# Two-queue head loads, PSUM-fed VectorE products, a later back transform and 490-wide tiles in a convolution-plus-MLP kernel

## The chip, the cores and the metric

The kernel runs on one core of one Trainium2 chip. The metric is the device time of the launch in microseconds. The engines are named as in the profile: PE (TensorE), DVE (VectorE), ACT (ScalarE), POOL (GpSimd), SP (SyncE, which here only issues DMAs). SBUF is the on-chip memory and PSUM the accumulator memory that PE writes, with banks of 512 fp32 values per partition.

## The reference

```python
def _attn_ref(x, v, pos_emb, w1, w2):          # x, v: (2, 12480, 128); pos_emb: (12480, 64)
    h_mlp = np.maximum(pos_emb @ w1, 0.0) @ w2
    window = np.exp(-0.01 * pos)[:, None]
    h_filt = h_mlp * window
    u = x * v
    Uf = np.fft.rfft(u, n=2 * S, axis=1)
    Hf = np.fft.rfft(h_filt, n=2 * S, axis=0)
    y = np.fft.irfft(Uf * Hf[None], n=2 * S, axis=1)[:, :S, :]
    return x * y

h = attn_out.reshape(24960, 128) @ w_in        # w_in: (128, 2048)
out = np.maximum(0.01 * h, h) @ w_out          # w_out: (2048, 128)
```

A causal convolution of length 12480 over 2 batches and 128 channels, gated by x, feeds an MLP over 24960 tokens. The large MLP weights arrive as float64.

## The kernel before

**MLP.** Each fp32 product is made from three fp32r matmuls of a high and a low part. A token tile (up to `WIDE` = 512 columns) runs `NF` = 16 steps over the hidden dimension. One step, called an iteration here, is `m1` (three matmuls into PSUM tile `mh`), the activation on ACT (`rh`) and the remainder on DVE (`rl`), and three steps later `m2` (three matmuls into `acc`). Tiles are 392 wide once, then 512, and two of 252 at the end: 50 tiles, 800 iterations. `mh` has three buffers.

**Convolution.** It is done as staged Fourier matmuls on 8 units (b, j): 2 batches times 4 blocks of the sequence, in the order (0,0), (1,0), (0,1), (1,1), (0,2), (1,2), (0,3), (1,3). Units with b = 0 also transform the filter. Each unit has two phases:

- `ConvA`: loads of x, v and pos_emb; POOL forms `uh` = x·v; PE transforms it in bursts; the result is copied out of PSUM and stored to a DRAM scratch `scr1`.
- `ConvB`, in 7 chunks (the last one small): load of `bin` from `scr1`; `up` (PE) makes the spectrum of u; for b = 0, `ep` and `hp` (PE) and `esg` (POOL) make the filter's spectrum; `mac` multiplies complex spectra, one term for j = 0, two for j = 1 and 3, five for j = 2; `dp` (PE) transforms the sum `pin` back, ACT copies it to `ct`, and it goes to scratch `scr2`. Spectra that later units need go through DRAM (`u`, `g`, `p`, loaded as `sp`).

A `mac` term is two 1024-wide products `t` of spectra in SBUF, one on POOL and one on DVE, an add of the earlier terms to the first on POOL where there are any, and a 512-wide difference (POOL) and sum (DVE) into `pin` or `pp`. `up` is therefore first copied from PSUM to `us` in SBUF by ACT. `dp` of chunk c-1 stands right after `up` and `hp` of chunk c.

**Fronts.** For each of 64 blocks of 392 tokens (384 in the last sequence block), `front` loads `cin`, makes y with matmuls (`yp`), gates it on DVE (`zt`), transposes it (`zp`), copies it on ACT to `zf` and then to `zh`, and POOL makes the low part `zl`. `finish` transposes the result back (`op`) and stores it.

**Order.** The Tile scheduler is off: each engine runs its instructions in program order. Unit (0,0) runs alone in a head, together with the conversion of the float64 weights (`from_float64`, `weights`). The other seven units are cut into pieces, and `pace` strews the pieces over the iterations: `cost` weighs the units, `windows` and `knots` turn the weights into an iteration range for each, and a piece is emitted when the iteration count has come that far. PE runs piece and iteration matmuls in one order, so a piece that waits holds back what stands behind it.

In the main part all conv matmuls use two PSUM banks, and a piece takes both:

```python
def pair():
    return psc["bank"](), psc["bank"]()
```

## Time and profile before

| | before |
|---|---|
| median of 3 runs | 2089.12 us (2085.14 to 2090.6) |
| profiled execution | 2086.52 us, span 2084.6 us |
| PE busy | 1793.9 us, 86% of the span |
| DVE, POOL, ACT busy | 1054.1, 960.2, 859.9 us |
| first `m1` matmul | 187.18 us |
| DMA | 290.61 MB, mean 139 GB/s |

The profiled execution's time is the span plus 1.92 us around it. The span falls into five stretches, cut where a unit's pieces begin: the head (unit (0,0) and weights, 0 to 187 us), the early units (1,0), (0,1), (1,1) to 729 us, the two units with j = 2 to 1424 us, the late units (0,3), (1,3) to 1869 us, and a tail with no convolution left.

### The profile page before, as it was taken

How to read it: one execution, taken by the hardware profiler on the slowest of the kernel's cores; microseconds unless marked ns; L12 is line 12 of the kernel's file. 1: busy time of each engine (PE TensorE's matmuls, PEld its weight loads, DVE VectorE, ACT ScalarE, POOL GpSimd, SP SyncE). 2: the span in 40 equal slices, each digit the busy share in tenths (PEclk: the TensorE clock that was granted, in tenths of full speed). 3: DMA queues.
4: the chain of work that ended last, by engine and by line, in shares of the span. 5: the costliest groups of instructions: out<-in, count | busy, mean ns of one | idle time of the engine just before them, and what ended most of it. 6: DMA issues, size and time to landing. Idle time of an engine off the chain costs nothing. (4 is left out here: it accounts for less than half of the span.)

```text
span 2084.6 us, 27982 instructions
## 1 busy us (share of the span) xinstructions
PE 1793.9 (86%) x9734; PEld 1258.0 (60%) x9734; DVE 1054.1 (51%) x1482; ACT 859.9 (41%) x1675; POOL 960.2 (46%) x618
## 2 busy tenths in 40 slices
PE   4566999998999899767779777769998899999999
PEld 3334767755676576444457444547765577667788
DVE  2673444455456444544454465555444445545665
ACT  1233544444444444222224232324443344445666
POOL 3232232166426511777773578872166624840000
PEclk9977999999999999887789888779999999999999
DMA  4685574566457454434425453433555356621100
GB/s 121 195 259 148 156 207 126 171 211 206 121 185 213 129 151 150 151 114 134 128 65 143 139 157 108 121 88 108 164 175 176 111 140 193 200 83 43 47 24 16
DMA packets 214034, 290.61 MB, mean 139 GB/s; under 512 B 30061, under 2 KB 138477, under 8 KB 213893
## 3 DMA queue, kind: packets, MB, share of 16 engines
q1 hardware_dynamic: 213893, 288.82, 46.5%
q8 instruction: 77, 1.26, 0.3%
q14 instruction: 64, 0.52, 0.1%
HBM read 181.23 MB, written 107.51 MB: 139 GB/s over the span
## 5 line engine op out<-in xcount | busy, mean ns | idle before, releaser
L745 DVE SCALAR_TENSOR_TENSOR rl<-mh,rh 128x512 fp32r<-128x512 f32 (+1 forms) x672 | 455.6, 685 | 545.7 <-ACT rh L744 545.3
L744 ACT ACTIVATE rh<-mh 128x512 fp32r<-128x512 f32 (+1 forms) x672 | 401.3, 597 | 490.8 <-PE mh L740 475.3
L738 PE MATMUL mh<-zh,w_in_h 128*128 128x512 f32 (+2 forms) x800 | 362.6, 453 | 73.4 <-DVE rl L745 72.2
L739 PE MATMUL mh<-zl,w_in_h 128*128 128x512 f32 (+2 forms) x800 | 319.9, 400 | 0.0
L740 PE MATMUL mh<-zh,w_in_l 128*128 128x512 f32 (+2 forms) x800 | 319.7, 400 | 0.0
L762 PE MATMUL acc<-rh,w_out_h 128*128 128x512 f32 (+2 forms) x800 | 318.8, 399 | 0.0
L763 PE MATMUL acc<-rl,w_out_h 128*128 128x512 f32 (+2 forms) x800 | 318.3, 398 | 0.0
L765 PE MATMUL acc<-rh,w_out_l 128*128 128x512 f32 (+2 forms) x800 | 318.0, 397 | 0.0
L731 POOL TENSOR_TENSOR zl<-zf,zh 128x392 fp32r<-128x392 f32 (+39 forms) x111 | 79.5, 731 | 487.4 <-ACT zh L730 487.1
L738 PEld LDWEIGHTS mh<-zh,w_in_h 128*128 128x128 f32 x800 | 154.1, 193 | 215.7 <-DVE rl L745 102.5
L432 PE MATMUL cv<-pin,mi 64*128 64x512 f32 (+1 forms) x416 | 133.9, 758 | 109.8 <-POOL pin L420 109.4
L420 POOL TENSOR_TENSOR pin<-t 128x512 f32<-128x512 f32 (+1 forms) x112 | 160.4, 1432 | 123.3 <-DVE t L416 107.4
L421 DVE TENSOR_TENSOR pin<-t 128x512 f32<-128x512 f32 (+1 forms) x112 | 87.6, 782 | 185.7 <-POOL t L418 176.0
L740 PEld LDWEIGHTS mh<-zh,w_in_l 128*128 128x128 f32 x800 | 155.6, 194 | 35.4
L763 PEld LDWEIGHTS acc<-rl,w_out_h 128*128 128x128 f32 x800 | 154.7, 193 | 36.1 <-DVE rl L753 0.2
L762 PEld LDWEIGHTS acc<-rh,w_out_h 128*128 128x128 f32 x800 | 154.9, 194 | 35.5
L765 PEld LDWEIGHTS acc<-rh,w_out_l 128*128 128x128 f32 x800 | 154.3, 193 | 35.8
L415 POOL TENSOR_TENSOR t<-us,sp 128x1024 f32<-128x1024 f32 (+1 forms) x63 | 139.4, 2212 | 63.0 <-ACT us L401 35.7
L739 PEld LDWEIGHTS mh<-zl,w_in_h 128*128 128x128 f32 x800 | 156.7, 196 | 16.6 <-DVE zl L731 0.3
L181 POOL TENSOR_TENSOR uh<-xt,vt 113x512 f32<-113x512 f32 x64 | 81.9, 1286 | 182.4 <-DMA vt<-in_v_dram 50.6
L432 PEld LDWEIGHTS cv<-pin,mi 64*128 64x128 f32 x416 | 46.3, 232 | 164.9 <-POOL pin L420 125.9
L436 ACT COPY ct<-cv 128x512 f32<-128x512 f32 (+1 forms) x104 | 53.7, 565 | 218.5 <-PE cv L432 213.8
(110 smaller groups left out, 2339.5 us busy)
## 6 DMA issues: line engine op xcount, KB each, us to landing
sp<-g SPq DMA_DIRECT2D x72, 512.0 KB
cin<-scr SPq DMA_DIRECT2D x64, 392.0 KB
scr<-ct SPq DMA_DIRECT2D x96, 256.0 KB
sp<-u SPq DMA_DIRECT2D x48, 512.0 KB
scr<-sp SPq DMA_DIRECT2D x128, 147.0 KB
bin<-scr SPq DMA_DIRECT2D x24, 768.0 KB
scr<-sp SPq DMA_DIRECT2D x64, 196.0 KB
xt<-in_x_dram SPq DMA_DIRECT2D x128, 96.0 KB
```

Of the source, the lines that this page charges most:

```text
L415: G(out=t1, in0=u, in1=g[:, 0:1, :].to_broadcast([R, 2, w]), op=ALU.mult)
L420: G(out=acc[:, 0], in0=t1[:, 0], in1=t2[:, 1], op=ALU.subtract)
L421: V(out=acc[:, 1], in0=t1[:, 1], in1=t2[:, 0], op=ALU.add)
L432: nc.tensor.matmul(p[jo][:, :w], mi2[rows, ri, :], pin[rows, ri, :w], start=(ri == 0), stop=(ri == 1))
L738: nc.tensor.matmul(hp, w_in_h[:, fs], zh, start=True, stop=False)
L739: nc.tensor.matmul(hp, w_in_h[:, fs], zl, start=False, stop=False)
L740: nc.tensor.matmul(hp, w_in_l[:, fs], zh, start=False, stop=True)
L744: nc.scalar.activation(out=rh, in_=hp, func=AF.Relu)
L745: nc.vector.scalar_tensor_tensor(out=rl, in0=hp, scalar=0.0, in1=rh, op0=ALU.max, op1=ALU.subtract)
L762: nc.tensor.matmul(ap, w_out_h[:, f, :], rh, start=(f == 0), stop=False)
L763: nc.tensor.matmul(ap, w_out_h[:, f, :], rl, start=False, stop=False)
L765: nc.tensor.matmul(ap, w_out_l[:, f, :], rh, start=False, stop=last and k >= LEAKY)
```

## The change

- **Tiles.** A tile is now made of whole groups of 98 (96 for j = 3) tokens, five to a tile: 392, then 490, for j = 3 480, and 192 at the end. There are 52 tiles and 832 iterations, with the same token columns in all.
- **Products.** The terms whose first factor is the fresh `up` (`first`: one, or two for j = 2) read it from PSUM: DVE does both products, POOL both halves of the join. In the remaining terms (`rest`) both factors are in SBUF: POOL does both products, and POOL the join, but for j = 2, where DVE does the sum. `us` is copied only where it is saved (j < 2).
- **PSUM.** A conv use takes one tile of two banks with one buffer in the main part (three in the head), and it is copied out by one ACT copy.
- **Back transform.** `dp(c-1)` stands behind the first rest term of chunk c (behind the first terms if there is no rest); `pin` has two buffers.
- **Fronts.** `zf` is gone: ACT copies `zh` from PSUM, and DVE makes `zl` from PSUM.
- **Loads.** `ConvA` loads x, v and pos_emb in granules of 8 positions instead of 4 (4, 12 and 16 in the head), into tiles that `ConvB` uses otherwise; one store for a burst instead of two. In the head a second queue, that of ACT, issues about 28 of the loads; the saves of `u` and `g` of unit (0,0) are kept back: six are issued in its chunks 4 to 6, the other eight behind the loads for the first fronts.
- **Pace.** New `cost`, and fewer pieces for most units. By the kernel's own arithmetic the iteration ranges of the stretches go from 233 (early), 227 (j = 2), 192 (late) and 148 (tail) to 202, 290, 200 and 140.
- **Instructions.** DMA issues of SP go from about 1494 to 1185.

```diff
+                self.granules = granules or [(8 * i, 8) for i in range(4)]
+                self.alloc = alloc or self.shared
...
+                i0, n = self.granules[g]
+                t = {}
+                for kind, src, d in (("p", pos_emb, FO), ("x", x[self.b], D), ("v", v[self.b], D)):
+                    if kind != "p" or self.hid:
+                        t[kind] = self.alloc(kind, g, n).rearrange("a (i d) -> a i d", d=d)
+                        load_tokens(t[kind], src, self.j, i0, n, q.get(kind, nc.sync))
+                self.got.append(t)
...
             def burst(self, c, i0, n):
                 e, r = self.e, rows_of(self.j)
                 uh = self.uh[c]
-                a = pair()
+                a = psc["pair"]().rearrange("p (w n) -> p w n", w=2)[:2 * KA]
...
-                o = spt(turn[0] % 4, [128, 1024])[:2 * KA, :2 * n * e].rearrange("k (w i e) -> k w i e", w=2, e=e)
+                o = spt(turn[0] % 5)[:2 * KA, :2 * n * e].rearrange("k (i w e) -> k w i e", w=2, e=e)
...
+                    m0 = 2 * (c * NI + i0)
+                    nc.sync.dma_start(out=scr1[self.b, self.j][m0:m0 + 2 * n].rearrange("m k e -> k m e"),
+                                      in_=o.rearrange("k w i e -> k i w e").rearrange("k i w e -> k (i w) e"))
...
+                self.first = [(g(0), "y")] + ([(g(1), "p")] if j == 2 else [])
+                self.rest = {0: [], 1: [(u(0), g(1), "y")], 3: [(u(0), g(3), "y")],
+                             2: [(u(1), g(1), "y"), (u(1), g(2), "p"), (u(0), g(2), "y")]}[j]
...
             def up(self, c):
...
-                us = self.env("us", [128, 2, 512], 1)
-                for ri in range(2):
-                    nc.scalar.copy(us[:R, ri, :w], p[ri][:R, :w])
                 if self.j < 2:
-                    self.late.append(lambda: nc.sync.dma_start(
-                        out=spec["u", self.b, self.j][c][:R, :1024].rearrange("p (r w) -> p r w", r=2)[:, :, :w],
-                        in_=us[:R, :, :w]))
-                return us
-
...
-                G, V = nc.gpsimd.tensor_tensor, nc.vector.tensor_tensor
-                G(out=t1, in0=u, in1=g[:, 0:1, :].to_broadcast([R, 2, w]), op=ALU.mult)
-                V(out=t2, in0=u, in1=g[:, 1:2, :].to_broadcast([R, 2, w]), op=ALU.mult)
+                    us = self.tile("us", 1024).rearrange("p (r w) -> p r w", r=2)
+                    nc.scalar.copy(us[:R, :, :w], p[:R, :, :w])
+                    self.save(("u", self.b, self.j), c, us)
+                return p[:R, :, :w]
+
+            def t01(self, c):
+                R, w = self.dims(c)
+                return [cpt(f"t{i}", 1024).rearrange("p (r w) -> p r w", r=2)[:R, :, :w] for i in range(2)]
+
+            def mult(self, c, eng, u, g):
+                R, w = self.dims(c)
+                t = self.t01(c)
+                for i in range(2):
+                    eng.tensor_tensor(out=t[i], in0=u[:R, :, :w], in1=g[:R, i:i + 1, :w].to_broadcast([R, 2, w]),
+                                      op=ALU.mult)
...
+            def join(self, c, t, acc, init, im):
+                R, w = self.dims(c)
+                G = nc.gpsimd.tensor_tensor
                 if init is not None:
-                    G(out=t1, in0=t1, in1=init[:R, :, :w], op=ALU.add)
-                yield
-                G(out=acc[:, 0], in0=t1[:, 0], in1=t2[:, 1], op=ALU.subtract)
-                V(out=acc[:, 1], in0=t1[:, 1], in1=t2[:, 0], op=ALU.add)
-                yield
+                    G(out=t[0], in0=t[0], in1=init[:R, :, :w], op=ALU.add)
+                G(out=acc[:R, 0, :w], in0=t[0][:, 0], in1=t[1][:, 1], op=ALU.subtract)
+                im(out=acc[:R, 1, :w], in0=t[0][:, 1], in1=t[1][:, 0], op=ALU.add)
 
...
-                p = pair()
+                p = psc["pair"]().rearrange("p (j w) -> p j w", j=2)
...
+                ct = cpt("ct", KC * D).rearrange("p (k d) -> p k d", d=D)
+                nc.scalar.copy(ct.rearrange("p (j h) d -> p j (h d)", j=2)[:, :H, :w], p[:, :H, :w])
...
-                    us = self.up(c)
-                    vals = {"U": us}
...
-                    if c >= 1:
-                        self.dp(c - 1, pin)
...
+                    acc = {"y": cpt("pin", 1024, 2).rearrange("p (r w) -> p r w", r=2)}
...
+                    rest = [o for t in self.rest for o in t[:2]]
+                    u = self.up(c)
+                    if self.defer and c > 3:
+                        for _ in range(2):
+                            self.defer.pop(0)()
+                    for i, (g, a) in enumerate(self.first):
+                        t = self.mult(c, nc.vector, u, vals[g])
                         yield
-                    pin = acc["y"]
+                        self.join(c, t, acc[a], init[a], nc.gpsimd.tensor_tensor)
+                        init[a] = acc[a]
+                        if i + 1 == len(self.first):
+                            self.load_bins(c + 2)
+                            if self.hid:
+                                if c + 1 < NCH:
+                                    self.ep(c + 1)
+                                    self.load_es(c + 2)
+                                yield
+                            if not self.rest:
+                                free(rest)
...
+                        t = self.mult(c, nc.gpsimd, vals[u], vals[g])
+                        yield
+                        self.join(c, t, acc[a], init[a],
+                                  nc.vector.tensor_tensor if self.j == 2 else nc.gpsimd.tensor_tensor)
+                        init[a] = acc[a]
+                        free([o for t in self.rest[i + 1:] for o in t[:2]])
+                        yield
+                        if i == 0 and c:
+                            self.dp(c - 1, pins.pop(c - 1))
+                            yield
+                    if not self.rest and c:
...
+                grain = [(0, 4), (4, 12), (16, 16)]
...
+                load_t(0, NI, (nc.sync, nc.scalar))
+                a0.load({"p": nc.scalar, "v": nc.scalar})
...
+                a0.load({"v": nc.scalar})
+                load_t(NI, 16 - NI, (nc.sync, nc.scalar))
...
+                a0.load({"v": nc.scalar})
...
+            load_front(0)
+            load_front(1)
+            for f in defer:
+                f()
...
-        psc["bank"] = psc["single"] = lambda: ps.tile([128, 512], F32, tag="cv", name="cv", bufs=2)
+        psc["pair"] = lambda: ps.tile([128, 1024], F32, tag="cv", name="cv", bufs=1)
+        psc["bank"] = psc["single"] = lambda: psc["pair"]()[:, :512]
...
+        groups = [(t, i) for t in range(total) for i in range(NI)]
+        cuts = list(range(NI, len(groups), GROUPS))
+        tiles = [groups[a:b] for a, b in zip([0] + cuts, cuts + [len(groups)])]
+        widths = [sum(size[t] // NI for t, _ in g) for g in tiles]
...
-            zf = sm.tile([128, 2 * NI * KA], F32, tag="zf", name="zf", bufs=1)
-            nc.scalar.copy(zf[:, :n].rearrange("p (i w a) -> p i w a", w=2, a=rows),
-                           zp.rearrange("p i (w a) -> p i w a", w=2)[:, :, :, :rows])
...
+                src = zp[:, i0:i0 + m].rearrange("p i (w a) -> p i w a", w=2)[:, :, :, :rows]
+                nc.scalar.copy(zh, src)
+                nc.vector.tensor_tensor(out=zl, in0=src, in1=zh, op=ALU.subtract)
...
-        cost = [0, 100, 125, 125, 170, 170, 140, 140]
+        cost = [0, 80, 110, 110, 215, 215, 125, 125]
```

POOL's rows in a full chunk of unit (0,2) before, from `esg` to the third term's join (`us` is the fresh spectrum, `sp` and `hs` other spectra, `t` the products):

```order
L356 TENSOR_TENSOR esg<-es,esp 128x4x64
L358 TENSOR_TENSOR esg<-es,esp 128x4x64
L415 TENSOR_TENSOR t<-us,sp 128x1024
L420 TENSOR_TENSOR pin<-t 128x512
L415 TENSOR_TENSOR t<-us,sp 128x1024
L731 TENSOR_TENSOR zl<-zf,zh 128x200
L731 TENSOR_TENSOR zl<-zf,zh 128x192
L420 TENSOR_TENSOR pp<-t 128x512
L415 TENSOR_TENSOR t<-sp 128x1024
L418 TENSOR_TENSOR t<-t,pin 128x1024
L420 TENSOR_TENSOR pin<-t 128x512
```

and after, from the joins of the two first terms to the second rest term's products:

```order
L425 TENSOR_TENSOR pin<-t_6805,t_6806 128x512
L426 TENSOR_TENSOR pin<-t_6805,t_6806 128x512
L425 TENSOR_TENSOR pp<-t_6833,t_6834 128x512
L426 TENSOR_TENSOR pp<-t_6833,t_6834 128x512
L363 TENSOR_TENSOR esg<-es,esp 128x4x64
L365 TENSOR_TENSOR esg<-es,esp 128x4x64
L416 TENSOR_TENSOR t_6900<-sp 128x1024
L416 TENSOR_TENSOR t_6901<-sp 128x1024
L424 TENSOR_TENSOR t_6900<-t_6900,pin 128x1024
L425 TENSOR_TENSOR pin<-t_6900,t_6901 128x512
L416 TENSOR_TENSOR t_6952<-sp,hs 128x1024
L416 TENSOR_TENSOR t_6953<-sp,hs 128x1024
```

The products of the two first terms are gone from POOL, which joins both in four 512-wide operations; of the rest terms it does two products each; `zl` is gone from it.

PE's rows of unit (1,1) before, from `up` of a chunk (L397) to `dp` of the chunk before it (L432):

```order
L397 MATMUL cv<-bin,mb 64x512 x4
L738 MATMUL mh<-zh,w_in_h 128x512
L739 MATMUL mh<-zl,w_in_h 128x512
L740 MATMUL mh<-zh,w_in_l 128x512
L762 MATMUL acc<-rh,w_out_h 128x512
L763 MATMUL acc<-rl,w_out_h 128x512
L765 MATMUL acc<-rh,w_out_l 128x512
L432 MATMUL cv<-pin,mi_91 128x512 x4
```

and after, the rows between that end with `dp` (L436); `up` stands above them, parted from them by one more iteration and a front's `yp`:

```order
L766 MATMUL mh<-zl,w_in_h 128x490
L767 MATMUL mh<-zh,w_in_l 128x490
L789 MATMUL acc<-rh,w_out_h 128x490
L790 MATMUL acc<-rl,w_out_h 128x490
L792 MATMUL acc<-rh,w_out_l 128x490
L765 MATMUL mh<-zh,w_in_h 128x490
L766 MATMUL mh<-zl,w_in_h 128x490
L767 MATMUL mh<-zh,w_in_l 128x490
L789 MATMUL acc<-rh,w_out_h 128x490
L790 MATMUL acc<-rl,w_out_h 128x490
L792 MATMUL acc<-rh,w_out_l 128x490
L436 MATMUL cv<-pin,mi_91 128x512 x4
```

One iteration stood between `up` and `dp`; now there are three.

## Rows read from the trace of the kernel before

**Rows 1.** Windows: length; busy PE, PEld, DVE, ACT, POOL; PE clock, DMA share, GB/s.

```profile
0.00:187.00 187.00, 102.53 (x642) 60.11 (x642) 95.90 (x184) 47.23 (x107) 62.61 (x61) 0.85 0.61 181
187.00:729.00 542.00, 515.27 (x2919) 360.23 (x2920) 272.31 (x363) 246.99 (x474) 227.21 (x155) 0.98 0.59 173
729.00:1424.00 695.00, 545.99 (x2664) 370.22 (x2663) 340.51 (x419) 227.90 (x435) 431.35 (x242) 0.86 0.41 125
1424.00:1869.00 445.00, 420.03 (x2379) 295.86 (x2378) 220.17 (x297) 200.70 (x386) 227.21 (x142) 0.98 0.51 155
1869.00:2084.60 215.60, 210.06 (x1135) 171.63 (x1134) 125.22 (x222) 137.09 (x274) 11.82 (x18) 1.00 0.12 34
```

**Rows 2.** Timeline of POOL over one chunk of unit (0,2).

```profile
1001.17 0.74 POOL L356 TENSOR_TENSOR esg<-es,esp 128x256 f32<-128x256 f32 x1 [5.37 <-ACT es L348]
...
1002.56 2.40 POOL L415 TENSOR_TENSOR t<-us,sp 128x1024 f32<-128x1024 f32 x1
...
1014.15 3.40 POOL L415 TENSOR_TENSOR t<-sp 128x1024 f32<-128x1024 f32 x1
...
1017.63 2.38 POOL L418 TENSOR_TENSOR t<-t,pin 128x1024 f32<-128x1024 f32 x1
...
1020.09 1.78 POOL L420 TENSOR_TENSOR pin<-t 128x512 f32<-128x512 f32 x1
...
1043.56 2.37 POOL L415 TENSOR_TENSOR t<-us,sp 128x1024 f32<-128x1024 f32 x1
```

**Rows 3.** Timeline of POOL, start of two successive chunks of unit (1,2).

```profile
1278.33 2.35 POOL L415 TENSOR_TENSOR t<-us,sp 128x1024 f32<-128x1024 f32 x1
...
1319.77 2.35 POOL L415 TENSOR_TENSOR t<-us,sp 128x1024 f32<-128x1024 f32 x1
```

**Rows 4.** Timeline of DVE in the chunk of rows 2.

```profile
1002.69 3.34 DVE L416 TENSOR_TENSOR t<-us,sp 128x1024 f32<-128x1024 f32 x1
...
1014.11 1.23 DVE L416 TENSOR_TENSOR t<-sp 128x1024 f32<-128x1024 f32 x1 [0.57 <-POOL pp L420]
```

**Rows 5.** Timeline of POOL, start of two successive chunks of unit (0,1).

```profile
462.45 2.41 POOL L415 TENSOR_TENSOR t<-us,sp 128x1024 f32<-128x1024 f32 x1
...
481.65 2.41 POOL L415 TENSOR_TENSOR t<-us,sp 128x1024 f32<-128x1024 f32 x1
```

**Rows 6.** Timeline of PE in the same chunk of unit (0,1), conv matmuls.

```profile
467.30 1.94 PE L397 MATMUL cv<-bin,mb 128*64 128x512 f32 x8
...
470.77 1.15 PE L374 MATMUL cv<-w,esg 64*64 64x128 f32 x32
...
475.80 1.99 PE L432 MATMUL cv<-pin,mi 64*128 64x512 f32 x8 [1.88 <-POOL pin L420]
...
478.45 1.09 PE L345 MATMUL cv<-mb,bin 128*64 128x128 f32 x16 [0.67 <-ACT ct L436]
```

**Rows 7.** Timeline of PE in the tail, one matmul of two successive iterations.

```profile
2046.04 0.40 PE L739 MATMUL mh<-zl,w_in_h 128*128 128x512 f32 x1
...
2047.44 0.40 PE L739 MATMUL mh<-zl,w_in_h 128*128 128x512 f32 x1
```

**Rows 8.** Groups by line, the matmuls of the fronts.

```profile
L715 PE MATMUL yp<-cin,gt 98*64 98x128 f32 x1024 | 72.3, 285 | 10.3 <-DMA cin<-scr 10.3
...
L722 PE MATMUL zp<-ident,zt 113*128 113x113 f32 x256 | 36.6, 266 | 0.8 <-DVE zt L717 0.8
```

**Rows 9.** Timeline of PE in the head.

```profile
52.69 0.61 PE L188 MATMUL cv<-ident,pos 113*128 113x113 f32 x2 [7.88 <-DMA pos<-in_pos_emb_dram]
...
182.28 1.98 PE L715 MATMUL yp<-cin,gt 98*64 98x128 f32 x16 [10.29 <-DMA cin<-scr]
```

**Rows 10.** Timeline of POOL in the head.

```profile
55.70 1.26 POOL L181 TENSOR_TENSOR uh<-xt,vt 113x512 f32<-113x512 f32 x1 [10.50 <-DMA vt<-in_v_dram]
```

**Rows 11.** Groups by form, two 512-wide DVE operations.

```profile
L753 DVE TENSOR_TENSOR rl<-sp,rh 128x512 fp32r<-128x512 f32 x96 | 66.7, 695 | 44.8 <-ACT rh L752 43.1
...
L717 DVE TENSOR_TENSOR zt<-yp,xm 113x512 f32<-113x512 f32 x64 | 43.9, 687 | 28.3 <-PE yp L715 27.1 <-DMA sp<-u 0.4 <-DMA scr<-sp 0.4
```

More of the change, by code (lines that the diff above doesn't have):

```diff
@@ L28 @@
 PAD = 1088
+GROUPS = 5
 @with_exitstack
@@ L136, in tile_conv_mlp @@
     psc = {}
-    def pair():
-        return psc["bank"](), psc["bank"]()
     with tc.manual_schedule():
@@ L148, in tile_conv_mlp, with spt, cpt, __init__ @@
         turn = [0]
[L150 to L151 removed]
+        def spt(i):
+            return cp.tile([128, 1024], F32, tag=f"sp{i}", name="sp")
+        kept = {}
+        for tag, n in (("us", 1024), ("hs", 1024), ("pp", 1024), ("ct", 1024), ("esp", 512), ("esg", 512)):
+            kept[tag] = const.tile([128, n], F32, name=tag)
+            nc.gpsimd.memset(kept[tag][32:64], 0.0)
+        def cpt(tag, n, bufs=1):
+            if tag in kept:
+                return kept[tag]
+            return cp.tile([128, n], F32, tag=tag, name=tag, bufs=bufs)
         class ConvA:
[L155 removed]
+            def __init__(self, b, j, granules=None, alloc=None, evac=None):
                 self.b, self.j = b, j
@@ L231, in run, with body @@
-            def run(self):
-                while self.loaded < 2:
-                    self.load()
-                first = self.prep(0)
-                for _ in first if self.hid else first or ():
+            def body(self):
+                if self.hid and self.j:
+                    load_win(self.j, nc.sync)
+                for i in range(2):
+                    if len(self.got) < 1 + i:
+                        self.load()
+                    yield
+                for _ in self.prep(0):
@@ L289, in __init__ @@
-                self.fresh = fresh
-                self.terms = terms
-                self.loads = []
-                if j == 3:
-                    self.loads.append(("p", b))
-                for t in terms:
-                    for o in t[:2]:
-                        if o not in ("U", fresh) and o not in self.loads:
-                            self.loads.append(o)
-                self.sp = {}
-            def pieces(self):
-                per = (4 if self.hid else 2) + 2 * len(self.terms)
-                return self.WAIT + 1 + NCH * per + 2
+                self.after, self.defer = after, defer
@@ new lines, in __init__, with dims @@
+                self.loads = [("p", b)] if j == 3 else []
+                for o in [t[0] for t in self.first] + [o for t in self.rest for o in t[:2]]:
+                    if o != self.fresh and o not in self.loads:
+                        self.loads.append(o)
+            def pieces(self):
+                per = (2 if self.hid else 0) + 2 * len(self.first) - 1 + 2 * len(self.rest) + 1
+                return self.WAIT + 1 + NCH * per + 3
+            def dims(self, c):
+                _, n, h = chunk(c)
+                return (128 if n > 1 else 64), h * D
@@ L431, in dp @@
                         rows = slice(64 * jo, 64 * jo + 64)
-                        nc.tensor.matmul(p[jo][:, :w], mi2[rows, ri, :], pin[rows, ri, :w],
+                        nc.tensor.matmul(p[:, jo, :w], mi2[rows, ri, :], pin[rows, ri, :w],
                                          start=(ri == 0), stop=(ri == 1))
-                ct = self.env("ct", [128, KC, D], 1)
-                for jo in range(H):
-                    nc.scalar.copy(ct[:, jo * h:jo * h + h, :].rearrange("p k d -> p (k d)"), p[jo][:, :w])
+                ct = cpt("ct", KC * D).rearrange("p (k d) -> p k d", d=D)
+                nc.scalar.copy(ct.rearrange("p (j h) d -> p j (h d)", j=2)[:, :H, :w], p[:, :H, :w])
                 def store():
@@ L670, in tile_conv_mlp, with headtile @@
+            hb = st.enter_context(tc.tile_pool(name="hb", bufs=1, reuse_waits="tile"))
+            defer = []
+            def headtile(tag, n):
+                return hb.tile([128, n], F32, tag=tag, name=tag, bufs=5)
+            nc.vector.tensor_scalar_mul(mi2, mi2, 4.0)
+            b0 = ConvB(0, 0, after=conv_a[1, 0].load, tile=headtile, defer=defer)
+            for i, _ in enumerate(b0.run()):
+                for _ in range(4 if i < 7 else 3):
+                    next(wprep, None)
                 if i == 12:
@@ L778, in finish @@
             whole = []
-            for t in range(total):
-                for kk, a, c, n in pieces_of(t):
+            for t in sorted({t for t, _ in tiles[k]}):
+                n = size[t] // NI
+                for kk, a, i0, m in parts[t]:
                     if kk == k:
@@ L800, in tile_conv_mlp @@
         ZB, DEEP = 3, 3
-        first = [next(pieces_of(t))[0] for t in range(total)]
+        first = [parts[t][0][0] for t in range(total)]
         ends, e = {}, NTL * NF
@@ L877, in do @@
                 next(fronts[t])
-        load_front(0)
-        load_front(1)
+        for _ in range(4):
+            step()
         run(front(0))
```

437 lines of the change are left out of this document (190 added, 247 removed).

## The prediction

> **What bounds the kernel now.** I read the windows first [rows 1]. [...] In the head PE works 103 of 187 us, no engine is full, and the DMA share is 0.61.
>
> POOL's timeline shows what holds j = 2 back. A full chunk of unit (0,2) starts with `esg`, and its first product starts 41.0 us before that of the next chunk [rows 2]; in unit (1,2) the distance is 41.4 us [rows 3]. The reader should look at the product times. POOL's takes 2.40 us at the chunk's start and 3.40 us later, and the DVE product of a pair takes 3.34 us where POOL came first and 1.23 us where DVE came first [rows 2, 4]. So two products from SBUF on these engines do not overlap; the second waits for the first. A term costs the sum of both engines' products, whoever has them. In the head, the rows to see are waits on loads: 7.88 us for `pos`, 10.50 us for `vt`, 10.29 us for `cin` [rows 9, 10].
>
> **Tiles.** An iteration 512 wide takes 1.40 us on PE [rows 7], so 1.34 us at 490 columns and 1.31 at 480. A front adds (72.3 + 36.6) / 64 = 1.70 us [rows 8], and the transposes of a finish are as many as those of `zp`, 0.57 us: 2.27 us for 392 tokens, 0.19 us for an iteration of 512 and 0.18 for one of 490. That makes 1.59 us before and 1.52 (j = 3: 1.49) after. All columns together stay the same, so the width costs nothing as such. It matters where iterations lie: the j = 2 stretch, in which PE waits anyway, takes 290 of them and not 227.
>
> - Early: 233 × 1.59 = 370 against 202 × 1.52 = 307, so 63 us less.
> - Late: 192 × 1.59 = 305 against 200 × 1.49 = 298, 7 us less: 438.
> - Tail: 116 × 1.40 and 32 of 252 columns at 0.69, 184.5, against 124 × 1.31 and 16 of 192 columns at 0.53, 171: 13.5 us less, 202.
>
> **j = 2.** `t0` and `t1` have one buffer each, so DVE's two products of a first term wait for POOL's last join and POOL's join waits for them: a chain over both engines.
>
> - A rest term: two POOL products at 2.37, the add 2.38, the difference with DVE's sum ahead of it 1.78 [rows 2, 3], 8.90 us; three make 26.7.
> - A first term: two products on DVE, then two 512-wide operations on POOL. No row has a product from PSUM. Its lower bound is the 1.23 us of the same product from SBUF [rows 4]; its upper bound is the 2.40 us that POOL takes. I take 1.23, since a 512-wide DVE operation takes 0.687 us with an operand in PSUM (`zt`) and 0.695 with both in SBUF [rows 11]. POOL's 512-wide operations are half of 2.37 each. So 2.46 + 2.37 = 4.83; two make 9.7.
> - `esg` twice 0.74 [rows 2], for b = 0 alone: 1.5.
>
> A chunk takes 37.8 us in unit (0,2) and 36.4 in (1,2), against 41.0 and 41.4; six full chunks each save 19 + 30 = 49 us. PE alone would need less: 12 pieces per chunk at 144.9 iterations / 130 pieces is 13.4 iterations or 20.4 us, and 6.2 us of conv matmuls [rows 6]. Outside these chunks more iterations lie: before, 57 of 141 pieces and 38 of 110 at 113.3 iterations for each unit, 85 iterations; after, 58 of 130 and 39 of 99 at 144.9, 122. That is 85 × 1.59 = 135 against 122 × 1.52 = 185, 50 us more. So 695 - 49 + 50 = 696 us: the stretch stays as long, with 63 more iterations in it.
>
> [...]
>
> **Early units.** A full chunk of unit (0,1) takes 19.2 us [rows 5]; PE alone 8 pieces at 0.84 iterations, 10.7 us, and 6.2 us of conv matmuls [rows 6], 16.9. The rest is the wait of `dp` for `pin` (1.88 us) and of `ep` for PSUM (0.67), on PE with iterations queued behind. After, `dp` stands two iterations further back and finds `pin` done. But POOL's chain becomes two products, add and join, 4.74 + 2.38 + 2.37, a first term, 4.83, and `esg`, 1.5: 15.8 us, while PE needs 6 × 0.84 × 1.52 + 6.2 = 13.9. The loss of 2 us stays. In (1,1), without `esg`, `hp` and `ep`, the chain is 14.3 us against 4 × 1.30 × 1.52 + 3.9 = 11.8 of PE, and before it was 6 × 1.23 × 1.59 + 3.9 = 15.6 of PE: a new loss of 2.5 us, 15 for six chunks. In (1,0) the eight saves kept back, 4 MB, run beside its loads; at the stretch's rate, 173 GB/s at a share of 0.59, a full DMA moves 293 GB/s, so they cost 0 to 14 us; I take 7. Early: 542 - 63 + 15 + 7 = 501.
>
> `zl` on DVE and the missing `zf` I cost at nothing: in these stretches DVE is busy half the time and ACT less [rows 1]. If that cover is gone, 0.7 us for each of some 100 pieces comes back.
>
> **Head.** Fewer, larger loads on two queues and fronts loaded ahead of the saves go at the three waits, 28.7 us together; there are shorter ones beside them, and ACT must first issue its share of loads before its first copy. Bounds: nothing (the data come no sooner) and 45. I take 30, near the three waits: 157.
>
> **Sum.** 157 + 501 + 696 + 438 + 202 = 1994 us of span, 1996 with the 1.92 us around it. The median of the runs lay 2.6 us over the profiled time, so 1999 us.
>
> **Rivals.**
>
> - *POOL is freed further.* If DVE's products ran beside POOL's rest terms, a chunk with j = 2 would fall to POOL's own 32.9 us (26.7 + 4.7 + 1.5): 12 × 4.9 = 59 us less, 1940; a head 15 us shorter still would give 1925. For it speaks that operations with a PSUM operand, such as `rl`, do not stretch in these rows; against it that the single `t` buffers tie the engines.
> - *Loads don't gain.* The head stays at 187, and the saves cost their 14 us: 2036; with light chunks 2 us longer than reckoned, 2065. For it: the DMA share of the head is already 0.61 as a mean. Against it: the waits are for few, small, early transfers.
> - *The single PSUM tile.* Every conv use waits in PE's order until the use before it has been copied out or multiplied; before, the first bank was free half a copy earlier, and `up` was released by ACT, not by DVE behind its `rl`. Outside the full j = 2 chunks there are some 190 uses; at 0.5 us of PE wait each 95 us come back, so from 0.5 us it is slower than before; at 0.6 us 2113. For it: `ep` already waits 0.67 us for `ct` [rows 6]. Against it: one or more iterations, 1.5 us each, lie between pieces in most places.
> - *No change.* The saving of 95 us goes to several of these at once and the time stays at 2089.
>
> **Chances.** What I forecast, 1965 to 2035: 0.55. POOL freed: 0.18. Loads don't gain, 2035 to 2080: 0.15. The PSUM tile: 0.08. No change: 0.04. So faster by over 0.3% (about what a measurement of this kernel can tell from no change) 0.88, within it 0.04, slower 0.08. The range 1930 to 2060 leaves out the low end of the second case, the top of the third, and the last two.
>
> **What would show it.** First `m1` matmul near 157 us. POOL's chunk starts in the j = 2 units 36 to 38 us apart, with gaps of 2.5 us while DVE multiplies, and DVE's products at 1.23 us. PE busy at above 95% in the other stretches, and no wait of `dp` for `pin` there. The forecast is wrong if the chunk distance is far from 37, if PE waits for DVE's products or ACT's copies at conv pieces over 0.5 us each, or if the product from PSUM takes nearer 2.4 us: then 48 × 1.17 = 56 us come back.

## The result, and the profile after

The changed kernel takes 2024.67 us (median of 4 runs, 2022.74 to 2026.45), 0.970 of the time before (95% interval 0.968 to 0.971). The forecast was 1999 us, in a range of 1930 to 2060.

The head of the page of the changed kernel, with the clock of PE in 40 slices:

```profile
span 2023.2 us, 27361 instructions
## 1 busy us (share of the span) xinstructions
PE 1760.4 (87%) x9932; PEld 1302.7 (64%) x9932; DVE 901.2 (45%) x1435; ACT 819.1 (40%) x1459; POOL 901.6 (45%) x608
...
PEclk9976989999999999888989998899999999999999
```

The span is 61 us shorter, 2023.2 against 2084.6, and PE is busy 87% of it. Where the time went is read from windows cut as in [rows 1] (length; busy time of PE, PEld, DVE, ACT, POOL; clock, DMA share, GB/s). The head ends with the first `m1` matmul, the other stretches with the last `dp` of a unit:

```profile
0.00:192.80 192.80, 104.83 (x643) 62.65 (x643) 98.28 (x183) 45.12 (x79) 58.43 (x64) 0.87 0.58 163
192.80:699.80 507.00, 457.23 (x2646) 324.04 (x2647) 197.82 (x293) 214.22 (x358) 205.43 (x148) 0.96 0.60 183
699.80:1387.30 687.50, 590.00 (x3151) 442.55 (x3149) 298.04 (x456) 248.43 (x445) 425.87 (x255) 0.92 0.43 131
1387.30:1817.10 429.80, 409.03 (x2403) 303.05 (x2401) 183.08 (x277) 182.92 (x324) 211.84 (x142) 0.99 0.53 160
1817.10:2023.20 206.10, 199.31 (x1098) 170.44 (x1096) 123.98 (x230) 128.45 (x253) 0.00 (x0) 1.00 0.13 36
```

Against 187, 542, 695, 445 and 215.6 us before: the main part gives 67 us, and the head takes 5.8 us more. In the j = 2 stretch PE is now busy 590 us and not 546, at a clock of 0.92 and not 0.86. In the early stretch it is busy 457 of 507 us, 90%, against 95% before.

POOL in a full chunk of unit (0,2) of the changed kernel, to hold against [rows 2]:

```profile
882.82 1.78 POOL L425 TENSOR_TENSOR pin<-t,t 128x512 f32<-128x512 f32 x1
...
887.82 1.29 POOL L425 TENSOR_TENSOR pin<-t,t 128x512 f32<-128x512 f32 x1 [3.22 <-DVE t L416]
889.07 1.28 POOL L426 TENSOR_TENSOR pin<-t,t 128x512 f32<-128x512 f32 x1
...
894.17 1.27 POOL L425 TENSOR_TENSOR pp<-t,t 128x512 f32<-128x512 f32 x1 [3.82 <-DVE t L416]
...
897.34 0.74 POOL L365 TENSOR_TENSOR esg<-es,esp 128x256 f32<-128x256 f32 x1
898.04 4.70 POOL L416 TENSOR_TENSOR t<-sp 128x1024 f32<-128x1024 f32 x2
902.71 2.37 POOL L424 TENSOR_TENSOR t<-t,pin 128x1024 f32<-128x1024 f32 x1
905.16 1.78 POOL L425 TENSOR_TENSOR pin<-t,t 128x512 f32<-128x512 f32 x1
```

and DVE in the same chunk:

```profile
885.32 2.36 DVE L416 TENSOR_TENSOR t<-cv,sp 128x1024 f32<-128x1024 f32 x2 [0.70 <-POOL pin L425]
...
891.75 2.35 DVE L416 TENSOR_TENSOR t<-cv,sp 128x1024 f32<-128x1024 f32 x2
```

Two joins (1.27 to 1.29 us each half), each behind a gap of 3.2 to 3.8 us in which DVE multiplies (two products in 2.36 us), then `esg`, then rest terms without a gap (two products 4.70, add 2.37, difference 1.78). This is the chain that the forecast added up, with gaps longer than its 2.46 us.

### The profile page after: what moved, and what is told of

Its sections match the earlier page's. It is cut to its first block, busy times and chain, and to the rows that moved or that the text cites. A ratio compares the mean times of both kernels' runs of the same rounds, so it can differ in the third digit from the quotient of the medians.

```text
span 2023.2 us, 27361 instructions
## 1 busy us (share of the span) xinstructions
PE 1760.4 (87%) x9932; PEld 1302.7 (64%) x9932; DVE 901.2 (45%) x1435; ACT 819.1 (40%) x1459; POOL 901.6 (45%) x608
## 3 DMA queue, kind: packets, MB, share of 16 engines
q8 instruction: 78, 1.28, 0.3%
## 4 chain that ended last, share of the span: by engine, by line
PE 58%; POOL 20%; DVE 8%; issue 7%; DMA 3%; ACT 2%; SPq 1%; ACTq 0%; POOLq 0%; DVEq 0%
POOL t L416 10%; PE mh L765 8%; PE mh L767 6%; PE mh L766 6%; PE acc L790 6%; PE acc L792 6%; PE acc L789 6%; PE cv L224 4%; POOL t L424 4%; PE cv L400 4%; DVE t L416 3%; PE cv L436 3%; PE yp L744 2%; POOL pin L425 2%; POOL pin L426 2%
## 5 line engine op out<-in xcount | busy, mean ns | idle before, releaser
L772 DVE SCALAR_TENSOR_TENSOR rl<-mh,rh 128x490 fp32r<-128x490 f32 (+3 forms) x704 | 458.8, 662 | 603.7 <-ACT rh L771 601.7
L771 ACT ACTIVATE rh<-mh 128x490 fp32r<-128x490 f32 (+3 forms) x704 | 406.4, 579 | 503.1 <-PE mh L767 483.7
L765 PE MATMUL mh<-zh,w_in_h 128*128 128x490 f32 (+4 forms) x832 | 367.1, 441 | 66.9 <-DVE rl L772 66.2
L766 PE MATMUL mh<-zl,w_in_h 128*128 128x490 f32 (+4 forms) x832 | 323.4, 389 | 0.0
L767 PE MATMUL mh<-zh,w_in_l 128*128 128x490 f32 (+4 forms) x832 | 323.2, 389 | 0.0
L790 PE MATMUL acc<-rl,w_out_h 128*128 128x490 f32 (+4 forms) x832 | 321.8, 387 | 0.0
L789 PE MATMUL acc<-rh,w_out_h 128*128 128x490 f32 (+4 forms) x832 | 321.0, 386 | 0.0
L792 PE MATMUL acc<-rh,w_out_l 128*128 128x490 f32 (+4 forms) x832 | 320.9, 386 | 0.0
L765 PEld LDWEIGHTS mh<-zh,w_in_h 128*128 128x128 f32 x832 | 161.5, 194 | 195.1 <-DVE rl L772 92.0
L425 POOL TENSOR_TENSOR pin<-t,t 128x512 f32<-128x512 f32 (+1 forms) x112 | 142.4, 1272 | 258.8 <-DVE t L416 250.8
L416 POOL TENSOR_TENSOR t<-sp 128x1024 f32<-128x1024 f32 (+1 forms) x84 | 178.1, 2141 | 9.6 <-issue 6.9
L789 PEld LDWEIGHTS acc<-rh,w_out_h 128*128 128x128 f32 x832 | 161.7, 194 | 26.7
L792 PEld LDWEIGHTS acc<-rh,w_out_l 128*128 128x128 f32 x832 | 160.8, 193 | 26.5
L400 PE MATMUL cv<-bin,mb 128*64 128x512 f32 (+1 forms) x416 | 109.4, 638 | 17.2 <-ACT hs L386 12.6
L436 PE MATMUL cv<-pin,mi 64*128 64x512 f32 (+1 forms) x416 | 109.3, 631 | 14.2 <-DVE t L416 13.1
```

What stands on the lines that cost most here:

```text
L400: nc.tensor.matmul(p[64 * jo:64 * jo + 64, ri, :w].rearrange("p (k d) -> p k d", d=D), mb[:, ri, :], t[:, jo * h:jo * h + h, self.off:], s ...
L416: eng.tensor_tensor(out=t[i], in0=u[:R, :, :w], in1=g[:R, i:i + 1, :w].to_broadcast([R, 2, w]), op=ALU.mult)
L425: G(out=acc[:R, 0, :w], in0=t[0][:, 0], in1=t[1][:, 1], op=ALU.subtract)
L765: nc.tensor.matmul(hp, w_in_h[:, fs], zh, start=True, stop=False)
L766: nc.tensor.matmul(hp, w_in_h[:, fs], zl, start=False, stop=False)
L767: nc.tensor.matmul(hp, w_in_l[:, fs], zh, start=False, stop=True)
```

## Experiments

All are edits of the changed kernel; each was timed against the kernel before, in 4 runs. Unit lengths, in us, run from one unit's last `dp` matmul to the next unit's, (1,0) from the first `m1`; the head ends there. Each is from one profiled execution.

| kernel | median us | ratio | head | (1,0) | (0,1) | (1,1) | (0,2) | (1,2) | (0,3) | (1,3) | tail |
|---|---|---|---|---|---|---|---|---|---|---|---|
| before | 2087.8 | 1 | 187.2 | 137.4 | 224.0 | 178.4 | 373.3 | 321.7 | 247.8 | 197.3 | 217.5 |
| changed | 2024.67 | 0.9697 | 192.8 | 130.5 | 207.5 | 169.0 | 362.8 | 324.7 | 227.5 | 202.3 | 206.1 |
| e1 SP only | 2032.9 | 0.9737 | 195.8 | 128.5 | 207.4 | 170.4 | 361.3 | 324.8 | 227.7 | 202.3 | 206.1 |
| e2 eight on ACT | 2031.69 | 0.9737 | 195.1 | 131.6 | 212.5 | 170.8 | 363.2 | 324.7 | 227.6 | 202.3 | 206.2 |
| e3 us last | 2028.29 | 0.9724 | 186.0 | 133.4 | 211.5 | 169.2 | 362.3 | 324.3 | 227.7 | 201.9 | 206.2 |
| e4 two pairs of t | 1981.83 | 0.9492 | 193.6 | 124.6 | 212.5 | 154.7 | 354.1 | 319.5 | 223.6 | 192.4 | 206.1 |
| e5 weights early | 2025.33 | 0.9717 | 194.2 | 123.6 | 212.7 | 169.0 | 361.7 | 324.7 | 227.8 | 202.1 | 206.2 |
| e6 us last in head | 2025.31 | 0.9713 | 189.5 | 127.0 | 212.7 | 171.0 | 363.1 | 324.7 | 227.6 | 202.3 | 206.2 |
| e7 together | 1973.77 | 0.9474 | 181.7 | 125.4 | 209.2 | 157.0 | 355.3 | 320.8 | 223.2 | 192.4 | 206.2 |
| e8 dp early | 2278.11 | 1.0933 | 200.3 | 136.7 | 240.1 | 214.9 | 402.2 | 373.9 | 257.1 | 243.3 | 206.2 |
| e9 light weights | 1997.76 | 0.9592 | 165.5 | 130.0 | 207.1 | 170.4 | 361.6 | 324.6 | 227.4 | 202.3 | 206.2 |
| e10 old cost | 2047.25 | 0.9822 | 192.3 | 152.8 | 220.4 | 178.8 | 352.7 | 310.8 | 228.6 | 203.1 | 206.2 |
| e11 from us | 2006.83 | 0.9629 | 191.8 | 114.4 | 196.2 | 168.9 | 363.7 | 326.5 | 230.4 | 208.8 | 206.3 |
| e12 best | 1953.43 | 0.9367 | 181.8 | 114.3 | 195.9 | 164.6 | 353.7 | 317.7 | 223.2 | 192.4 | 206.1 |

**The head: load order (e1, e2).**

```diff
-                load_t(0, NI, (nc.sync, nc.scalar))
-                a0.load({"p": nc.scalar, "v": nc.scalar})
+                load_t(0, NI, (nc.sync, nc.sync))        # e1; e2 leaves these two lines as they were
+                a0.load()
...
-                load_win(0, nc.scalar)
-                a0.load({"v": nc.scalar})
+                load_win(0, nc.sync)
+                a0.load()
```

and so for every other load on ACT's queue in the head.

> The changed kernel with all loads of the head issued by SP; nothing on ACT's queue. Theory A (ACT spends 2.5 to 29.0 us on issuing 25 loads, and its first copy, at 30.4, is what PE waits 16.6 us for): ACT's first copy comes at about 15 to 18 us, the first m1 matmul 5 to 12 us earlier than 192.8, time 2013 to 2020. Theory B (the head waits for data that one queue brings no sooner): first m1 at 193 or later, up to 205, time 2025 to 2037.

> The changed kernel with only the first eight loads on ACT's queue (half of the first tt, the first pos and v); all later loads of the head on SP. Theory A: ACT's first copy at about 15 us, the first m1 at 178 to 185, time 2010 to 2017, the best of the two load orders. Theory B: first m1 within 3 us of 192.8, time 2022 to 2028.

What theory A was read from, PE in the changed kernel:

```profile
30.70 1.20 PE L211 MATMUL s<-w1bd,pts 128*113 128x128 f32 x4 [16.55 <-ACT pts L207]
```

and ACT there, from the last of its DMA issues (ACTq) to its first copy:

```profile
28.42 0.55 ACTq L98 DMA_DIRECT2D v<-in_v_dram  x1
29.00 1.28 ACT L207 ACT_TABLE_LOAD   x1 [29.00 <-DMA tt<-in_cf_dram]
30.30 0.35 ACT L207 COPY pts<-s 128x226 f32<-128x226 f32 x1
```

ACT did come free earlier: its first copy stood at 12.5 us (e1) and 13.9 us (e2) and not at 30.3, and the first bursts ran at 22 and 18 us, not at 33. But ConvA's last burst ended at 77 us (74 in the changed kernel), and the head ended 2 to 3 us later. Theory A's forecast fell, and e1 came as theory B had it; e2's head did too, while its time lies above both ranges. The two runs do not show that ACT's issues cost nothing, for they moved a second thing: SP, with all these loads to issue, came to the first weight block `wi` at 49.7 (e1) and 46.4 us (e2) and not at 43.8. Its conversion stands on DVE ahead of a step of ConvA, and there PE now waits, in e1 (and so in e2, 13.18 and 14.61 us):

```profile
54.34 0.29 DVE L120 TENSOR_SCALAR fa<-wi 128x256 uint32<-128x256 uint32 x1 [12.41 <-DMA wi<-in_moe_w_in_dram]
...
55.35 0.64 PE L204 MATMUL s<-ident,p 113*128 113x113 f32 x2 [13.85 <-DVE t L213]
```

One wait went, and another took its place. What ACT's issues cost, and what two queues are worth against one, these two runs leave open.

**The head: what sets it (e3, e5, e6, e9).** In e3 `us` is copied behind the products, in e6 in the head alone:

```diff
                         t = self.mult(c, nc.vector, u, vals[g])
+                        if i == 0:                 # e6: if self.defer is not None:
+                            self.keep(c, u)        # the copy to us and its save, taken out of up
                         yield
```

> The changed kernel with the ACT copy of the fresh spectrum to us written behind DVE's two products of it. In the head DVE's products wait 23.9 us in all for that copy, in the whole kernel 55.6 us. If that wait is on the path (theory A: the head's chunk is a loop of PE, ACT, DVE and the weight conversion on DVE), about 1 us for each of seven chunks in the head goes, and some of 21 in the main part: first m1 183 to 188, time 2012 to 2019. If it only fills time that the loop waits anyway (theory B): within 4 us of 2024.7.

> The changed kernel with us copied behind DVE's products in the head alone. With the copy moved in all units the first m1 came at 186.0, but the main part took as much longer. If that loss came from the main part's own copies (ACT, with the activations queued behind it, waiting for DVE): first m1 at 186, time 2016 to 2020. If what the head gains is always lost again because the main part's first unit waits for something else: time 2022 to 2028.

e5 brings the weights forward, and e9 leaves out six of the eight DVE operations of each conversion. The edit of e5:

```diff
                 load_t(NI, 16 - NI, (nc.sync, nc.scalar))
+                next(wprep)
...
-                    if i >= 12:
+                    if i >= 6:
                         next(wprep, None)
```

> The changed kernel with the first weight loads issued behind the second granule and the weight steps begun at piece 6 of ConvA, not 12. Theory C (the head ends when the conversion of the float64 weights on DVE ends, 161.7 us in the changed kernel as 161.3 before, and everything else of the head hides behind it): the first conversion starts 10 to 20 us before 48.2, the last wcs 5 to 15 us before 161.7, the first m1 at 178 to 188, time 2010 to 2020. Theory B (the loads of x, v and pos set the head): they come later behind 1 MB of weights, first m1 at 195 to 200, time 2027 to 2032.

> The changed kernel with six of the eight DVE operations of each weight conversion left out (the weights, and so the output, are not the reference's), all steps and loads in place. Theory D (in the head a chunk of ConvB and a block of weights, 8.2 us alone, follow each other instead of overlapping, 15.7 us together): 16 conversions lose about 2.3 us each, of which those inside ConvA are partly hidden: first m1 25 to 37 us earlier than 192.8, at 156 to 168, time 1988 to 2002. Theory B (arrival of loads sets the head): first m1 at 186 or later, time over 2016.

e9 alone moved the head as expected: 27.3 us, to 165.5, and the time by 27 us. With e5 the conversion began at 41.2 us and not 48.2, and the last `wcs` (DVE's last step of a block of weights) came at 155.6 and not 161.7, but ConvA ended 8 us later and the first `m1` stood at 194.2. So both strands count, not the place of the weights alone: theory C as I put it (all else hides behind the conversion) fell, theory D held, and theory B's ranges were missed by 1 to 2 us. The chain of the changed kernel's head shows the loop; the columns are start, length, engine, tile and line:

```profile
98.80 2.36 DVE t L416 x2
101.39 1.40 DVE fa L128
...
107.71 0.44 DVE wo L131
108.28 1.19 PE wcp L620 x4
109.47 3.64 PE cv L400 x8
113.13 1.02 ACT us L404
114.25 2.36 DVE t L416 x2
116.84 1.39 DVE fs L124
...
124.53 1.19 PE wcp L620 x4
125.72 2.98 PE cv L400 x8
```

A chunk's `up` (L400) stands on PE behind `wcp` (L620) of the weights, which waits for DVE's conversion; the conversion stands on DVE behind the chunk's products, which wait for `us` and `up`. One chunk and one block of weights take 15 to 16.2 us (98.80 to 114.25 is one round) one after the other; weights alone took 8.2 us a block (84.6 to 92.8 us). e3 and e6 took links out of this loop, 6.8 and 3.3 us of head, but their times did not fall (ratios 0.9724, 0.9703 to 0.9745, and 0.9713, 0.9698 to 0.9727), so that of e3's theories A was right on the head and B on the time, and for e6 the second reading held. Unit (0,1) took 4 to 5 us more; beside it, in e3 unit (1,0) took 2.9 us more, in e6 3.5 us less and (1,1) 2.0 us more. The window of (0,1) from 410 to 525 us, in the changed kernel and then in e6:

```profile
410.00:525.00 115.00, 95.62 (x652) 63.95 (x653) 39.63 (x54) 44.31 (x71) 81.90 (x58) 0.96 0.62 203
```

```profile
410.00:525.00 115.00, 96.90 (x601) 65.53 (x599) 40.60 (x55) 42.73 (x69) 83.35 (x61) 0.90 0.59 194
```

The clock differs, 0.96 and 0.90, in a unit whose program is the same in both. Over the whole unit it is 0.98 and 0.94. Why it ran lower there stays open.

**The chain in the main part (e4).** A second pair of product tiles, used in turn:

```diff
+                flip[0] ^= self.defer is None
+                g = extra if flip[0] and self.defer is None else cpt      # extra: tiles xt0, xt1
-                return [cpt(f"t{i}", 1024).rearrange("p (r w) -> p r w", r=2)[:R, :, :w] for i in range(2)]
+                return [g(f"t{i}", 1024).rearrange("p (r w) -> p r w", r=2)[:R, :, :w] for i in range(2)]
```

> The changed kernel with a second pair of product tiles t0 and t1 in the main part, used in turn. Theory A (a chunk with j = 2 is a chain over POOL and DVE, tied by the single pair): DVE's second first-term product runs beside POOL's first join, and the first product starts beside POOL's last difference, so the chunk distance falls from 39.3 and 37.3 us to 35 to 37 and 33 to 35, 30 to 40 us for twelve chunks: time 1985 to 1995. Theory B (PE's order, with up and ep behind the single PSUM tile, sets the distance): the distance stays within 1 us, time 2018 to 2026.

The time fell by 43 us, more than theory A's 30 to 40, but not at the place it named. From the first `up` to the seventh, a j = 2 chunk takes 37.1 and 35.7 us on average, against 38.6 and 36.7, just above the ranges of theory A: 14 us of the 43 lie in these units. As much, 14.3, lies in unit (1,1), 9.9 in (1,3) and 5.9 in (1,0), while (0,1) took 5.0 more. POOL in (1,1), changed kernel:

```profile
617.61 1.27 POOL L425 TENSOR_TENSOR pin<-t,t 128x512 f32<-128x512 f32 x1 [2.47 <-DVE t L416]
...
628.59 1.26 POOL L426 TENSOR_TENSOR pin<-t,t 128x512 f32<-128x512 f32 x1
632.39 1.27 POOL L425 TENSOR_TENSOR pin<-t,t 128x512 f32<-128x512 f32 x1 [2.53 <-DVE t L416]
```

and with two pairs:

```profile
614.91 1.28 POOL L432 TENSOR_TENSOR pin<-t,t 128x512 f32<-128x512 f32 x1
...
625.77 1.29 POOL L433 TENSOR_TENSOR pin<-xt,xt 128x512 f32<-128x512 f32 x1
627.01 1.29 POOL L432 TENSOR_TENSOR pin<-t,t 128x512 f32<-128x512 f32 x1
```

The gap of 2.53 us in front of the join is gone, and the distance of the joins goes from 14.8 to 12.1 us. In the j = 2 chunks gaps of 3 to 4 us stay (3.17 and 3.96 us in one of unit (0,2)): there DVE's products stand behind `rl` and `zt` operations, of which in the changed kernel's chunk above one `rl` waited 1.10 us for ACT's `rh` and the `zt` 0.43 us for PE's `yp`.

**The place of `dp` (e8).**

```diff
                     rest = [o for t in self.rest for o in t[:2]]
+                    if c:
+                        self.dp(c - 1, pins.pop(c - 1))
+                    yield
                     u = self.up(c)
...
-                        if i == 0 and c:
-                            self.dp(c - 1, pins.pop(c - 1))
```

> The changed kernel with dp of chunk c-1 written behind hp of chunk c and ahead of its up, so that it stands right behind the last join of its pin. Theory A (the later place lets POOL end before PE arrives, and in units with j = 2 up and the next first products stand behind dp in the chain): PE's wait of dp for pin goes from 13 us back toward 109 us, each full j = 2 chunk is 3 to 5 us longer, the others 2 to 3: time 2080 to 2130. Theory B (the place of dp matters little, since the chain of POOL and DVE sets the chunk anyway): 2024 to 2045.

Theory A, by much more than I had given it: 253 us, to a time far above its range. PE's wait of `dp` in e8:

```profile
PE cv L436 <- POOL pin L425: 226.7, 45, 8.8
```

and all its waits on products and `pin` in the changed kernel, of which the 13 us that I had put down to `pin` are for the PSUM tile that DVE's products hold:

```profile
PE cv L436 <- DVE t L416: 13.1, 6, 2.6
...
PE cv L436 <- POOL pin L425: 1.0, 2, 0.7
```

Of the seven units of the main part, the six with a rest term grew by 30 to 49 us each, (1,0), which has none, by 6. With one PSUM tile, `up` and the first products stand behind this `dp`, so its wait lengthens the chain too: 46 us for a j = 2 chunk. This is an earlier place than that of the kernel before, where `dp` waited 109.4 us in all, so it bounds what the move is worth and does not measure it.

**Iterations moved (e10).**

```diff
-        cost = [0, 80, 110, 110, 215, 215, 125, 125]
+        cost = [0, 100, 125, 125, 170, 170, 140, 140]
```

> The changed kernel with the old table of costs: by the kernel's arithmetic 248, 241, 203 and 140 iterations in the early, j = 2, late and tail stretches instead of 202, 290, 200, 140. Theory A (iterations are free in the j = 2 chunks, where POOL and DVE set the distance, and cost 1.52 us elsewhere): j = 2 chunk distances stay within 1 us of 39.3 and 37.3; the early stretch grows by 50 to 70 us, the j = 2 stretch shrinks by 20 to 32; time 2050 to 2068. Theory B (PE work, not POOL and DVE, sets j = 2): its stretch shrinks by 49 x 1.52 = 74 us, as much as the early one grows; time 2020 to 2030.

Theory A, with a smaller cost in the early stretch than its 50 to 70 us and a time 3 us below its range: the early stretch grew by 45 us, the j = 2 stretch shrank by 24.0, and the chunks stayed at 38.3 and 36.3 us. The new table is worth 23 us of the 63.

**PSUM or SBUF as the source (e11).**

```diff
-                if self.j < 2:
-                    us = self.tile("us", 1024).rearrange("p (r w) -> p r w", r=2)
-                    nc.scalar.copy(us[:R, :, :w], p[:R, :, :w])
-                    self.save(("u", self.b, self.j), c, us)
-                return p[:R, :, :w]
+                us = self.tile("us", 1024).rearrange("p (r w) -> p r w", r=2)
+                nc.scalar.copy(us[:R, :, :w], p[:R, :, :w])
+                if self.j < 2:
+                    self.save(("u", self.b, self.j), c, us)
+                return us[:R, :, :w]
```

> The changed kernel with the fresh spectrum copied to us in all units and DVE's first-term products reading us instead of PSUM. It frees the single PSUM tile after one ACT copy and not after two or four products. Theory A (the chain of POOL and DVE is on the path, and the PSUM tile is not): a product stays at 1.22 us while POOL is idle, the copy adds up to 1 us per chunk: time 2024 to 2045. Theory B (conv matmuls wait for the PSUM tile until DVE has multiplied): PE's waits shrink, time 1990 to 2018. If DVE reading SBUF meets POOL's operations, products of 3 us and more appear and the time is over 2045.

Theory B, by 18 us, all of it in units (1,0) and (0,1), where `us` is copied anyway: 16.1 and 11.3 us less. With j = 2 and 3, where the copy is new, it is 1 to 6.5 us more a unit. In the units with j = 3 that is not the copy alone. There POOL adds two spectra from SBUF while DVE does its second product, and all twelve full adds became longer once DVE's two operands came from SBUF as well, in the changed kernel and then in e11:

```profile
L424 POOL TENSOR_TENSOR t<-t,sp 128x1024 f32<-128x1024 f32 x12 | 28.4, 2368 | 65.8 <-DVE t L416 65.8
```

```profile
L424 POOL TENSOR_TENSOR t<-t,sp 128x1024 f32<-128x1024 f32 x12 | 39.5, 3296 | 68.0 <-DVE t L416 59.7 <-issue 8.4
```

That is 11 us for both units, which grew by 9.4 together. So it is here that the product from PSUM pays: POOL's add runs beside it in 2.37 us and not 3.30. `dp` in unit (1,0), changed kernel:

```profile
265.37 1.99 PE L436 MATMUL cv<-pin,mi 64*128 64x512 f32 x8 [2.18 <-DVE t L416]
...
274.44 3.62 PE L436 MATMUL cv<-pin,mi 64*128 64x512 f32 x8 [2.18 <-DVE t L416]
```

and with products from `us`:

```profile
268.65 1.99 PE L436 MATMUL cv<-pin,mi 64*128 64x512 f32 x8
...
277.69 1.99 PE L436 MATMUL cv<-pin,mi 64*128 64x512 f32 x8
```

The PSUM tile is held until DVE has multiplied, PE waits 1.8 to 2.2 us for it in five of seven chunks, and some of these matmuls then run longer: 3.62 us at a granted clock of 0.54 (274.4 to 278.1 us), 1.99 us at 1.00 (265.3 to 267.4 us). Over the unit the clock is 0.92, against 0.96 in e11. In unit (0,1) it is `ep` that waits: PE stands idle for 17.6 us in front of it in the changed kernel and for 3.4 us in e11, though `up` then waits 8.4 us for `hs` and not 1.7.

**Together (e7, e12).** e7 is e4 with e2, e5 and the copy of e6; e12 reads `us` for j < 2 besides.

> The changed kernel with the second pair of product tiles (main part), us last in the head, only eight loads on ACT's queue and the weights early. If the effects add (theories A for j = 2 and C for the head): first m1 at 173 to 183, time 1960 to 1973. If the head's gain is lost again in the early units: 1976 to 1984, as with the second pair alone.

> The kernel with the second pair of product tiles, us last in the head, eight loads on ACT's queue and the weights early (1973.8 us), and in the main part's units with j < 2, where us is copied anyway, DVE's products read us and not PSUM; units with j = 2 and 3 read PSUM as in the changed kernel. With the products from us everywhere, units (1,0) and (0,1) were 16 and 11 us shorter, (1,1) equal, the j = 2 and 3 units 1 to 6 us longer. If that came from the single PSUM tile, held until DVE had multiplied, the first two units are 114 to 118 and 196 to 200 us here and the time is 1945 to 1960. If the second pair of product tiles had already taken that wait away (unit (1,0) was 125 us with it), time 1965 to 1975.

e7's time of 1973.77 us lies just above the range for effects that add, its head of 181.7 us inside it. In the head, which none of e2, e5 and e6 shortened by more than 3.3 us alone, the three together give 11.1. The traces fit that e2 and e5 each moved one wait to another place: in e2 PE waited 14.61 us in ConvA behind the conversion of `wi`, in e5 21.50 us for ACT's first copy, which ACT came to at 35.4 us, behind its loads; in e7 the conversion starts at 29.0 us, no wait of PE in ConvA is over 5 us but that for its first load, and the last `wcs` comes at 141.6. e12, at 1953.43 us, came as expected if the gain of e11 was the PSUM tile's: it is 0.937 of the time before (0.933 to 0.941), and unit (1,0) is 16 us shorter than in the changed kernel.

## Why the prediction was right, and where a step failed

- **The failed step is the head's.** The sum went "near the three waits" and took 30 us off; the head took 5.8 us more, so 36 us too little, and outside its own bounds. The three waits of [rows 9, 10] were real, but taking them for what ends the head was wrong. What its end hung on is the loop of weight blocks and chunks: e9, which made the blocks lighter, took 27.3 us out, and e5, which only moved them forward, nothing. The change starts the conversion 11.4 us sooner (48.2 us against 59.6), but the first `up` comes at 94.4 us and not at 82.3, and the last `wcs` at 161.7 us (161.3 before). From there to the first `m1` it is 31.1 us, 25.9 before: the third of the waits, 10.29 us for `cin`, grew. No run tried why; the rival "Loads don't gain" had the head nearly right, at 187 us.

```profile
188.41 1.98 PE L744 MATMUL yp<-cin,gt 98*64 98x128 f32 x16 [14.05 <-DMA cin<-scr]
```

- **The main part was forecast at 1837 us and took 1830.4**: early 507.0 (501), j = 2 687.5 (696), late 429.8 (438), tail 206.1 (202). The gain is 67 us there, where 60 was forecast; e10 shows 23 of it to be the table's. That the sum is so near is in part luck, since errors of both signs met: the early stretch holds the cost of the PSUM tile, 27 us by e11, which the sum put at nothing, so its other terms were some 20 us too long; for j = 2 see the next point. The sum let PE's work alone set the gains of the early, late and tail stretches from fewer or narrower iterations; no run shows that nothing else counts there, and PE was busy 90, 95 and 97% of them in the changed kernel.
- **Chunk with j = 2.** Forecast 37.8 and 36.4 us; 38.6 and 36.7 on average. Mis-sized were the 512-wide POOL operation, 1.28 and not 1.19 us, and the gap for DVE's products, 2.5 to 3.8 us and not 2.46. For unit (1,2) I took the 41.4 us before from one pair of chunks [rows 3]; from its first `up` to its seventh the mean was 37.6, so chunks gave 5 us there and not 30, and the unit grew by 3. In unit (0,2) the mean went from 40.9 to 38.6. Both units' chunks gave 19 us where 49 was forecast, and what lies outside them cost 11 us where 50 was forecast. The two errors cancel: that the stretch came within 9 us of the forecast is luck.
- **The product from PSUM.** All of its 1024-wide products with `sp`, in the changed kernel:

```profile
L416 DVE TENSOR_TENSOR t<-cv,sp 128x1024 f32<-128x1024 f32 x108 | 127.1, 1219 | 102.9 <-POOL pin L426 60.5 <-ACT us L404 31.3 <-PE cv L400 9.5
```

and from `us`, in e11:

```profile
L416 DVE TENSOR_TENSOR t<-us,sp 128x1024 f32<-128x1024 f32 x108 | 127.4, 1221 | 124.4 <-POOL pin L426 75.4 <-ACT us L403 37.5 <-DMA sp<-g 5.3
```

1.219 and 1.221 us: no cost of the PSUM source, as the two rows of [rows 11] had it. That operations with a PSUM operand do not stretch, which the prediction names with its first rival, fits `rl` from `mh` in the kernel before (0.691 us in the median, 0.694 at most, while DVE's sum of two `t` in SBUF took 0.692 in the median and up to 1.772), and is borne out by POOL's adds (2.37 us beside products from PSUM, 3.30 in e11 beside products from SBUF).
- **(1,1)** was given a new loss of 15 us from the single `t` tiles; e4 took 14.3 us back there.
- **The rival of a freer POOL** did not come: even with two pairs of `t` a chunk takes 37.1 and 35.7 us, not 32.9.
- **The rival of the single PSUM tile** was right in kind in two units: PE's waits of about 2 us for DVE's products in (1,0) were the prediction's own sign of being wrong, and PE was busy 90% of the early stretch, not above 95%. It cost 27 us (e11), not the 95 that it needed to decide.
- The rival of no change speaks of a saving of 95 us; the sum itself saves 90.
- `zl` on DVE, the 490-wide tiles and the 7 us for the saves kept back were not tried alone, and no run puts the old products back. So of the main part's 67 us, 23 are shown to be the table's; how the rest divides among the products, the place of `dp`, the tiles and the fronts is not shown.

## What to carry to other kernels

Where two engines pass tiles to and fro, add up the chain tile by tile, with the buffers that tie it, and then double that buffer: the chain gave a chunk to 0.8 and 0.3 us here, and the second pair another 43 us. Take what the chunk took before as a mean over all chunks, not from one pair. Here a product read from PSUM took what one from SBUF took (1.219 and 1.221 us), and POOL's add beside it kept its 2.37 us, but the product held the banks (PE waited 1.8 to 2.2 us for them in unit (1,0)): in two of the three units where a copy was made anyway, reading the copy was 16.1 and 11.3 us faster. A wait taken out of a head can come back at another load (in e1 16.55 us for ACT went and 13.85 us behind the load of `wi` came) while a longer strand (here the conversion of weights, in one order with the chunks on three engines) ends last: leave part of that strand out once, and see whether the end moves.
